# A fused attention and gated-MLP decode step: output rows spread over 128 partitions, value tiles loaded one place later, one store per queue, fifteen tiny loads

## The chip, the cores and the metric

The kernel runs on one core of a Trainium2 chip. The metric is the time of one execution on the device in microseconds (us). Three runs of the kernel before took 204.35, 204.86 and 204.87 us, median 204.86. The profile is of one execution whose span is 204.9 us. All times in this document count from the start of that span unless something else is said.

## What is computed

Eight tokens (B = 8) go through a layer norm. From the result `xn` two branches are made and multiplied, and the input is added:

```python
def A(x, k_cache, v_cache, wq, wo):     # attention, window W = 2048 of Sk = 8192
    q = (x @ wq)                        # 32 heads of 128
    k, v = the last W rows of the caches, 8 heads, each shared by 4 query heads
    p = softmax(q k^T * 128 ** -0.5)
    return (p v) @ wo
def B(x, w_gate, w_up, w_down):
    return (sigmoid(x @ w_gate) * (x @ w_up)) @ w_down
xn = layernorm(x)
out = x + A(xn) * silu(B(xn))           # [8, 1, 512], bf16
```

The bytes decide the size of the job. The windows of the two caches are 2 x 8 tokens x 8 heads x 2048 rows x 256 B = 67 MB, the weights another 14 MB. The profile counts 81.01 MB read from HBM.

## The kernel before

**Loads.** Nearly all loads are issued from SP's queue (`q0`), in one fixed order. A list `todo` holds them, and `pump` issues the head of the list while its pool has a free buffer: `kpool` with 5 buffers (tag "k") and `vpool` with 4 (tag "v"). `free(tag)` gives a buffer back after the last instruction that reads it, and pumps. The order is: `w_gate`, `w_up`, `w_down` (in the v pool, 1792 KB each), two halves of `wq` (in the k pool, 2 MB each), and then the cache tiles. A cache tile is 2 MB: one token, four heads, 128 partitions of 16 KB. There are 16 key tiles and 16 value tiles (two for each token); here they are called k0 to k15 and v0 to v15. The constant `AHEAD` (L165) places value tile n behind key tile n + AHEAD. With AHEAD = 3 the order is k0 k1 k2 k3 v0 k4 v1 ... k15 v12 v13 v14 v15. Last comes `wo`, 4 MB, 32 rows of 1 KB for each partition, in five loads: rows 0 to 4 by `load_side` (L110), and rows 5-14, 15-22, 23-28 and 29-31 by `load_rows` (L97). `load_side` views its 128 rows as 8 x 16, with the 8 outermost, so partition p holds another block of `wo` than in the other four loads. The work after it makes up for that, see below.

The framework gives DMAs from SP and ACT eight completion semaphores in turn. A DMA that takes a semaphore again first waits, on its issuing queue, until the DMA eight places before it has landed completely.

**Compute.** For each token, 16 steps (`k_transposes`, L392) turn the key tiles by TensorE (L401) and copy them out of PSUM by VectorE (L406). `scores` (L413) multiplies them with the query. `row_max`, `stat_rows`, `spread_max` and `p_transposes` make the softmax one token later, `values` (L514) multiplies with the value tiles two tokens later, and `combine`, `normalise` (L541) and `turn` (L571) bring each token's attention output into the layout that the last product needs, three tokens later. The order on TensorE is written by hand in `tasks` (L586 to L608): with 16 half steps for each token, the values of tile 0 of token b - 2 stand in half steps 1 to 8 of token b, those of tile 1 in half steps 7 to 14. So v(2b - 4) is multiplied while k(2b) is turned. After the loop stands a tail for the last tokens (L610 to L637), and then `fin` (L641): 128 matmuls of 128x128 with the rows of `wo` in order, into four blocks of 32 PSUM partitions. Two VectorE operations (L656, L658) multiply with the gate and add x, and four stores (L660) write the result.

**Layouts that the change touches.** `Z` = 32 is the block of partitions for each quarter j of the 512 output columns. In the kernel before, token b's output row is partition 32 j + b: the 8 tokens are the first 8 of 32. `hT_sb`, `oP_sb` and the identity `ident[:B, :Z]` carry this layout. In `normalise` two VectorE operations write the same product in two orders, `oB` for rows 5 to 31 and `oA` for rows 0 to 4 (the `load_side` rows), and `turn` has one matmul for each.

Of the kernel before, what the change touches and what calls it, by code (L numbers as in the profile page):

```python
# [10 lines left out]
def kernel(  # L11
# [13 lines left out]
    nc = tc.nc  # L25
    P = 128
    B, _, D = A_x.shape
    _, Hkv, Sk, Dh = A_k_cache.shape
    Hq = A_wq.shape[1] // Dh
# [19 lines left out]
    bf16 = mybir.dt.bfloat16  # L49
    f32 = mybir.dt.float32  # L50
    AF = mybir.ActivationFunctionType
    ALU = mybir.AluOpType
# [5 lines left out]
    kpool = ctx.enter_context(tc.tile_pool(name="kpool", bufs=5))  # L58
# [3 lines left out]
    consts = ctx.enter_context(tc.tile_pool(name="consts", bufs=1))  # L62
    work = ctx.enter_context(tc.tile_pool(name="work", bufs=1))
    small = ctx.enter_context(tc.tile_pool(name="small", bufs=2))
# [16 lines left out]
    q0, q1 = nc.sync, nc.scalar  # L81
    k_tiles = {}
    v_tiles = {}
    room = {"k": 5, "v": 4}
# [12 lines left out]
    def load_rows(w, tag, per, r0, r1, name):  # L97
        t = pools[tag].tile([P, r1 - r0, w.shape[1]], bf16, name=name, tag=tag)
        q0.dma_start(  # L99
            out=t[:], in_=w.rearrange("(p r) n -> p r n", r=per)[:, r0:r1, :]  # L100
        )
        return t
# [1 line left out]

    A = 8
    SD = 5

    def load_side(w, per):  # L110
        t = kpool.tile([P, SD, w.shape[1]], bf16, name="wo_sb", tag="k")
        q0.dma_start(
            out=t[:].rearrange("p r n -> p (r n)"),
            in_=w.rearrange("(e a r) n -> a e (r n)", a=A, r=per)[
                :, :, : SD * w.shape[1]
            ],
        )
        return t

    weights = {}  # L120
    todo = []

    def later(tag, f):
        todo.append((tag, f))
# [11 lines left out]
    def want_rows(name, w, tag, per, r0, r1):  # L136
        def f():
            t = load_rows(w, tag, per, r0, r1, name)
            for r in range(r0, r1):
                weights[(name, r)] = t[:, r - r0, :]  # L140

        later(tag, f)
# [4 lines left out]

        later(tag, f)

    def want_side():  # L150
        def f():
            t = load_side(A_wo, RT)
            for r in range(SD):
                weights[("wo_sb", r)] = t[:, r, :]

        later("k", f)

    RT = 32
    want_rows("wg_sb", B_w_gate, "v", KT, 0, KT)
    want_rows("wu_sb", B_w_up, "v", KT, 0, KT)  # L160
    want_rows("wd_sb", B_w_down, "v", FT, 0, FT)
    for i in range(2):
        want_rows("wq_sb", A_wq, "k", KT, 2 * i, 2 * i + 2)
    order = [(b, i) for b in range(B) for i in range(NQ)]
    AHEAD = 3  # L165
    for n in range(len(order) + AHEAD):
        if n < len(order):
            want_cache(k_tiles, A_k_cache, "k", *order[n])
        if n >= AHEAD:
            want_cache(v_tiles, A_v_cache, "v", *order[n - AHEAD])  # L170
    want_side()
    for t0, t1 in ((SD, 15), (15, 23), (23, 29), (29, RT)):
        want_rows("wo_sb", A_wo, "k", RT, t0, t1)

    x_bf = work.tile([B, D], bf16, name="x_bf")
# [3 lines left out]
    ident = consts.tile([P, P], bf16, name="ident")  # L179
# [8 lines left out]
        out=perm[:].rearrange("k (l p) -> k l p", l=G),  # L188
        in_=ident[:].rearrange("k (p l) -> k l p", l=G),
# [13 lines left out]
        out=rstd[:], in_=mv[:, 1:2], func=AF.Sqrt, bias=eps_t[:], scale=1.0  # L203
# [4 lines left out]
        out=xn_bf[:],  # L208
        in0=x_f[:],
# [7 lines left out]
    for kt in range(KT):  # L217
        nc.tensor.transpose(
            out=xnT_ps[:, kt, :],
            in_=xn_bf[:].rearrange("b (p kt) -> b kt p", kt=KT)[:, kt, :],  # L220
# [4 lines left out]

    Z = 32
    NB = D // P


    M0 = Z - rep  # L230
# [5 lines left out]
    hT_sb = work.tile([P, FT, Z], bf16, name="hT_sb")  # L236
    nc.vector.memzero(hT_sb[:])
    oP_sb = work.tile([P, RT, Z], bf16, name="oP_sb")
    nc.vector.memzero(oP_sb[:])

    NDQ = Dh // RT
    band = consts.tile([P, NDQ], bf16, name="band")
    pick = consts.tile([P, RT], bf16, name="pick")
    with nc.allow_low_precision(reason="zeros and a one"):
        nc.vector.reduce_sum(
            out=band[:], in_=ident[:].rearrange("k (q t) -> k q t", t=RT), axis=AX.X
        )
        nc.vector.reduce_sum(
            out=pick[:], in_=ident[:].rearrange("k (q t) -> k t q", t=RT), axis=AX.X
# [5 lines left out]
    for k in range(F // FC):  # L255
        g_ps = ps_t.tile([B, FC], f32, name="g_ps", tag="t")
        for kt in range(KT):
            nc.tensor.matmul(  # L258
                g_ps[:],
                lhsT=xnT_sb[:, kt, :],  # L260
                rhs=weights[("wg_sb", kt)][:, k * FC : (k + 1) * FC],
                start=(kt == 0),
                stop=(kt == KT - 1),
# [7 lines left out]
    for k in range(F // FC):  # L271
        u_ps = ps_t.tile([B, FC], f32, name="u_ps", tag="t")
        for kt in range(KT):
            nc.tensor.matmul(
                u_ps[:],
                lhsT=xnT_sb[:, kt, :],
                rhs=weights[("wu_sb", kt)][:, k * FC : (k + 1) * FC],
                start=(kt == 0),
                stop=(kt == KT - 1),
            )  # L280
        nc.vector.tensor_tensor(
            out=h_bf[:B, k * FC : (k + 1) * FC],
            in0=sigs[k],
            in1=u_ps[:],
            op=ALU.mult,
        )
    free("v")
    hT_ps = ps_m.tile([P, FT, B], bf16, name="hT_ps", tag="m")
    for t in range(FT):
        nc.tensor.transpose(  # L290
            out=hT_ps[:, t, :],
            in_=h_bf[:B, :F].rearrange("b (p t) -> b t p", t=FT)[:, t, :],
            identity=ident[:B, :B],
        )
    nc.vector.tensor_copy(out=hT_sb[:, :, :B], in_=hT_ps[:])

    b_ps = ps_s.tile([P, P], f32, name="b_ps", tag="s")
    for t in range(FT):
        for j in range(NB):
            nc.tensor.matmul(  # L300
                b_ps[Z * j : Z * (j + 1), :],
                lhsT=hT_sb[:, t, :],
                rhs=weights[("wd_sb", t)][:, j * P : (j + 1) * P],
                start=(t == 0),
                stop=(t == FT - 1),
# [9 lines left out]
    x4_ps = ps_m.tile([P, P], f32, name="x4_ps", tag="m")  # L315
    for j in range(NB):
        nc.tensor.matmul(
            x4_ps[Z * j : Z * (j + 1), :],
            lhsT=ident[:B, :Z],
            rhs=x_bf[:, j * P : (j + 1) * P],  # L320
            start=True,
            stop=True,
            tile_position=(0, Z * j),
            skip_group_check=True,
        )
# [5 lines left out]
    for h in range(Hq):  # L331
        for kt in range(KT):
            nc.tensor.matmul(  # L333
                qT_ps[:, h * B : (h + 1) * B],
                lhsT=weights[("wq_sb", kt)][:, h * Dh : (h + 1) * Dh],
                rhs=xnT_sb[:, kt, :],
                start=(kt == 0),
                stop=(kt == KT - 1),
            )
    for g in range(Hkv):  # L340
        nc.vector.tensor_copy(  # L341
            out=qm_sb[:, :, g, M0 : M0 + rep],
            in_=qT_ps[:, rep * g * B : rep * (g + 1) * B].rearrange(
                "p (hh b) -> p b hh", hh=rep
            ),
# [11 lines left out]
    for i in range(NQ):  # L357
        nc.vector.tensor_copy(
            out=turn_rows[:].rearrange("k (i j l r) -> k i j l r", i=NQ, j=NJ, l=G)[
                :, i  # L360
            ],
            in_=ident[:].rearrange("k (l j i r) -> k i j l r", i=NQ, j=NJ, l=G)[:, i],
        )
        nc.vector.reduce_sum(
            out=sel_den[:, i * Hh : (i + 1) * Hh].rearrange("k (l r) -> k l r", l=G),
            in_=ident_f[:].rearrange("k (l j i r) -> k i l r j", l=G, j=NJ, i=NQ)[:, i],
            axis=AX.X,
        )
    for e in range(2):
        nc.vector.reduce_sum(  # L370
            out=sel_out[:, e, :].rearrange("k (i h) -> k i h", i=NQ),
            in_=ident_f[:].rearrange(
                "k (i m e h) -> k e i h m", i=NQ, m=NJ // 2, e=2
            )[:, e],
# [9 lines left out]
    oT_ps = [m_ps[:, x, 168 : 168 + Hq] for x in range(2)]  # L384
    oP_ps = [m_ps[:, x, 200 : 200 + RT] for x in range(2)]
# [5 lines left out]
    row = {}  # L391
    inv = {}  # L392
# [148 lines left out]
    def normalise(b):  # L541
        o = row.pop(b)
        for e in range(2):
            nc.tensor.matmul(  # L544
                oT_ps[b % 2],
                lhsT=o[:, e, :],
                rhs=sel_out[:, e, :],
                start=(e == 0),
                stop=(e == 1),
            )  # L550

        HA = A // NDQ
        oB = small.tile([P, Hq * NDQ], bf16, name="oB")
        oA = small.tile([P, Hq * NDQ], bf16, name="oA")
        f = inv.pop(b)
        for to in (
            oB[:].rearrange("p (e s q) -> p e s q", s=HA, q=NDQ),
            oA[:].rearrange("p (s q e) -> p e s q", s=HA, q=NDQ),
        ):
            nc.vector.tensor_tensor(  # L560
                out=to,
                in0=oT_ps[b % 2]
                .rearrange("p (e s) -> p e s", s=HA)
                .unsqueeze(3)
                .to_broadcast([P, Hq // HA, HA, NDQ]),
                in1=f[:].rearrange("p (e s) q -> p e s q", s=HA),
                op=ALU.mult,
            )
        row[b] = oB, oA

    def turn(b):  # L571
        oB, oA = row.pop(b)
        for t, t0, t1 in ((oB, SD, RT), (oA, 0, SD)):
            nc.tensor.matmul(  # L574
                oP_ps[b % 2][:, t0:t1],
                lhsT=t[:],
                rhs=pick[:, t0:t1],
                start=True,
                stop=True,
            )  # L580
        nc.scalar.copy(out=oP_sb[:, :, b], in_=oP_ps[b % 2])  # L581

    for b in range(B):
        pb = b - 1 if b >= 1 else None
# [56 lines left out]
    def fin(t0, t1):  # L641
        for t in range(t0, t1):
            for j in range(NB):
                nc.tensor.matmul(  # L644
# [11 lines left out]
    nc.vector.tensor_tensor(out=prod[:], in0=gg_sb[:], in1=fin_ps[:], op=ALU.mult)  # L656
    y_bf = work.tile([P, P], bf16, name="y_bf")
    nc.vector.tensor_tensor(out=y_bf[:], in0=prod[:], in1=x4_f[:], op=ALU.add)  # L658
    for j in range(NB):
        (q0, q1)[j % 2].dma_start(  # L660
            out=out.flatten_outer_dims()[:, j * P : (j + 1) * P],
            in_=y_bf[Z * j : Z * j + B, :],
        )


# [28 lines left out]
```

## Time and profile before

| what | value |
|---|---|
| median of 3 runs | 204.86 us (204.35 to 204.87) |
| the profiled execution | span 204.9 us, from the first to the last instruction |
| HBM read | 81.01 MB, 395 GB/s over the span |
| DMA queue of SP | 6072 packets, 81.01 MB, 95.2% of 16 DMA engines' span |
| TensorE matmul busy | 164.6 us (80%) |
| VectorE busy | 128.1 us (63%) |
| ScalarE busy | 37.9 us (18%) |
| last `fin` matmul ends, issue of the last store ends | 201.5 us, 202.9 us |

How to read it: the share of a DMA queue is the time its packets took, over 16 engines times the span. Every load of 128 partitions is cut into 16 equal parts, one for each DMA engine, and each engine reports its own landing. So the trace has, beside the instructions, 16 landing times for one load; where this document says "the first engine" and "the last engine" of a load, it means the earliest and the latest of these.

### The profile page before, as it was taken

The numbers are of one execution on the slowest core, as the hardware profiler recorded it, in microseconds if no ns is written. First come the engines' busy times: TensorE is split into PE (matmuls) and PEld (weight loads), VectorE is DVE, ScalarE is ACT, GpSimd is POOL, SyncE is SP. The second block draws the span as 40 slices with busy tenths as digits, with TensorE's granted clock in tenths as the row PEclk, the third lists the DMA queues.
The fourth block names the chain that finished last, engine by engine and source line by source line (L and its number), as shares of the span: only waits on it lengthen the run. The fifth ranks groups of instructions, "written<-read, shape, count | busy, mean of one in ns | idle before, by whom it ended". The sixth has DMA issues, their size and how long they took to land.

```text
span 204.9 us, 5273 instructions
## 1 busy us (share of the span) xinstructions
PE 164.6 (80%) x2374; PEld 112.4 (55%) x2374; DVE 128.1 (63%) x246; ACT 37.9 (18%) x97; POOL 1.3 (1%) x9
## 2 busy tenths in 40 slices
PE   0496067999789989998969898999698998778542
PEld 0144066777656656566646665666466665457431
DVE  4824007899788678677947795778277967704201
ACT  5130000002501500510060006001500060070100
POOL 2000000000000000000000000000000000000000
PEclk9999555999999999999999999999799999999855
DMA  6999999999999999999999999999999999999940
GB/s 225 423 442 427 432 419 438 425 427 432 429 435 413 441 422 432 429 429 438 419 432 432 419 440 414 441 419 429 438 419 438 425 435 419 390 345 239 352 170 5
DMA packets 6141, 81.34 MB, mean 397 GB/s; under 512 B 736, under 2 KB 744, under 8 KB 1128
## 3 DMA queue, kind: packets, MB, share of 16 engines
q1 hardware_dynamic: 6072, 81.01, 95.2%
q8 instruction: 18, 0.29, 0.5%
q14 instruction: 3, 0.02, 0.0%
q10 hardware_dynamic: 48, 0.01, 0.0%
HBM read 81.01 MB, written 0.01 MB: 395 GB/s over the span
## 4 chain that ended last, share of the span: by engine, by line
DMA 54%; PE 36%; DVE 4%; ACT 2%; SPq 1%; issue 1%
DMA k_sb<-in_A_k_cache_dram 43%; PE kT_ps L401 20%; DMA wo_sb<-in_A_wo_dram 11%; PE o_ps L520 6%; PE s_ps L420 5%; PE pT_ps L483 3%; DVE kT_sb L406 3%; ACT p_buf L469 2%; SPq L99 1%; PE m_ps L500 1%; ACT L469 1%; PE m_ps L544 0%; PE m_ps L455 0%; DVE own L493 0%; DVE st L435 0%
## 5 line engine op out<-in xcount | busy, mean ns | idle before, releaser
L406 DVE COPY kT_sb<-kT_ps 128x1024 bf16<-128x1024 bf16 x128 | 87.5, 696 | 27.0 <-PE kT_ps L401 25.3
L401 PE MATMUL kT_ps<-perm,k_sb 128*128 128x128 bf16 x1024 | 79.4, 225 | 6.0 <-DMA k_sb<-in_A_k_cache_dram 6.0
L401 PEld LDWEIGHTS <-k_sb 128*128 128x128 bf16 x1024 | 60.6, 101 | 27.7 <-issue 20.5
L520 PE MATMUL o_ps<-v_sb,pT_sb 128*32 128x256 bf16 x512 | 41.1, 278 | 0.3 <-DVE pT_sb L488 0.3
L420 PE MATMUL s_ps<-kT_sb,qm_sb 128*32 128x512 bf16 x256 | 26.0, 397 | 0.5 <-DVE kT_sb L406 0.5
L520 PEld LDWEIGHTS <-pT_sb 128*32 128x32 bf16 x512 | 18.0, 96 | 9.2 <-issue 1.5
L469 ACT ACTIVATE p_buf<-s_ps,nb 32x512 bf16<-32x512 f32 x32 | 21.7, 678 | 0.5
L488 DVE COPY pT_sb<-pT_ps 128x1024 bf16<-128x1024 bf16 x16 | 10.9, 686 | 8.5 <-PE pT_ps L483 8.5
L483 PE MATMUL pT_ps<-turn_rows,p_buf 128*128 128x128 bf16 x128 | 10.9, 230 | 2.7 <-ACT p_buf L469 2.7
L463 ACT COPY nb<-m_ps 128x1 f32<-128x1 f32 x8 | 1.3, 160 | 60.6 <-PE m_ps L455 60.6
L536 ACT COPY o_sb<-o_ps 128x256 f32<-128x256 f32 x8 | 3.0, 372 | 51.0 <-PE o_ps L520 51.0
L483 PEld LDWEIGHTS <-p_buf 128*128 128x128 bf16 x128 | 9.2, 150 | 4.6 <-ACT p_buf L469 3.2
L420 PEld LDWEIGHTS <-qm_sb 128*32 128x32 bf16 x256 | 6.6, 93 | 7.5 <-issue 0.9
L333 PE MATMUL qT_ps<-xnT_sb,wq_sb 128*128 128x8 bf16 x128 | 3.7, 168 | 7.1 <-DMA wq_sb<-in_A_wq_dram 7.1
L258 PE MATMUL g_ps<-wg_sb,xnT_sb 128*8 128x448 bf16 x16 | 5.4, 526 | 3.1 <-DMA wg_sb<-in_B_w_gate_dram 3.1
L581 ACT CAST oP_sb<-m_ps 128x32 bf16<-128x32 f32 x8 | 2.4, 301 | 29.0 <-PE m_ps L574 25.2
L333 PEld LDWEIGHTS <-wq_sb 128*128 128x128 bf16 x128 | 3.6, 104 | 7.3 <-DMA wq_sb<-in_A_wq_dram 7.3
L644 PE MATMUL fin_ps<-wo_sb,oP_sb 128*32 128x128 bf16 x128 | 4.4, 309 | 3.8 <-DMA wo_sb<-in_A_wo_dram 3.3
L341 DVE CAST qm_sb<-qT_ps 128x32 bf16<-128x32 f32 x8 | 0.9, 183 | 10.2 <-PE qT_ps L333 10.2
L500 PE MATMUL m_ps<-own,ones_sq 128*128 128x32 f32 x16 | 3.3, 287 | 4.7 <-DVE own L493 4.6
L500 PEld LDWEIGHTS m_ps<-own,ones_sq 128*128 128x128 f32 x16 | 2.4, 188 | 7.1 <-DVE own L493 7.1
L644 PEld LDWEIGHTS <-oP_sb 128*32 128x32 bf16 x128 | 3.3, 138 | 4.7 <-issue 4.2
(68 smaller groups left out, 83.3 us busy)
## 6 DMA issues: line engine op xcount, KB each, us to landing
k_sb<-in_A_k_cache_dram SPq DMA_DIRECT2D x16, 2048.0 KB, 29.7
v_sb<-in_A_v_cache_dram SPq DMA_DIRECT2D x16, 2048.0 KB, 22.7
wq_sb<-in_A_wq_dram SPq DMA_DIRECT2D x2, 2048.0 KB
wg_sb<-in_B_w_gate_dram SPq DMA_DIRECT2D x1, 1792.0 KB, 7.3
wu_sb<-in_B_w_up_dram SPq DMA_DIRECT2D x1, 1792.0 KB, 11.1
wd_sb<-in_B_w_down_dram SPq DMA_DIRECT2D x1, 1792.0 KB
wo_sb<-in_A_wo_dram SPq DMA_DIRECT2D x1, 1280.0 KB, 19.3
wo_sb<-in_A_wo_dram SPq DMA_DIRECT2D x1, 1024.0 KB
```

The lines of the kernel that those rows point to most:

```text
L258: nc.tensor.matmul(g_ps[:], lhsT=xnT_sb[:, kt, :], rhs=weights[("wg_sb", kt)][:, k * FC : (k + 1) * FC], start=(kt == 0), stop=(kt == KT - 1),
L333: nc.tensor.matmul(qT_ps[:, h * B : (h + 1) * B], lhsT=weights[("wq_sb", kt)][:, h * Dh : (h + 1) * Dh], rhs=xnT_sb[:, kt, :], start=(kt = ...
L401: nc.tensor.transpose(out=kT_ps[:, c, :], in_=k_sb[:, j * CU + h * CH + c, :], identity=perm[:],)
L406: nc.vector.tensor_copy(out=kT[(b, u)][:, h * CH : (h + 1) * CH, :], in_=kT_ps[:])
L420: nc.tensor.matmul(s_ps[b][NR * l : NR * (l + 1), :], lhsT=qm_sb[:, b, i * G + l, o : o + Z], rhs=t[:, :, PG * l : PG * (l + 1)], start=(u ...
L469: nc.scalar.activation(out=p_buf[b % 2][rows, :, l, :], in_=s[rows, :].rearrange("k (c p) -> k p c", p=PG), func=AF.Exp, bias=nb[rows, :], ...
L483: nc.tensor.transpose(out=pT_ps[:, c, :], in_=p_buf[b % 2][:, :, :, h * CH + c].rearrange("k p l -> k (p l)"), identity=turn_rows[:],)
L488: nc.vector.tensor_copy(out=pT[b][:, h * CH : (h + 1) * CH, :], in_=pT_ps[:])
L500: nc.tensor.matmul(den_ps[b % 2], lhsT=ones_sq[:], rhs=own[:], start=True, stop=True)
L520: nc.tensor.matmul(o_ps[rows, b % 2, :].rearrange("k (e d) -> k e d", e=2), lhsT=pT[b][:, c, rows], rhs=v[:, m, c], start=(c == 0), stop=( ...
L536: nc.scalar.copy(out=o[:], in_=o_ps[:, b % 2, :].rearrange("k (e d) -> k e d", e=2))
L644: nc.tensor.matmul(fin_ps[Z * j : Z * (j + 1), :], lhsT=oP_sb[:, t, :], rhs=weights[("wo_sb", t)][:, j * P : (j + 1) * P], start=(t == 0), ...
```

## The change

Five edits:

- `load_side` is gone. `wo` comes in four loads of 12, 9, 7 and 4 rows, all by `load_rows`. `normalise` writes one order (`oB`), with one VectorE operation where there were two, and `turn` has one matmul where there were two.
- The tokens' output rows are spread: token b of quarter j stands on partition 32 j + 4 b, where it was 32 j + b (`SB` = 4). A small constant `spread` takes the place of `ident[:B, :Z]`.
- With that, quarters j and j + 1 are one pattern of 16 partitions with step 4, and each of the two queues (SP and ACT) issues one store of 2 x 8 x 128 where it issued two of 8 x 128.
- AHEAD is 4: the order of the tiles is k0 k1 k2 k3 k4 v0 k5 v1 ... k15 v11 v12 v13 v14 v15.
- Fifteen new loads, called probes here, stand in SP's order between the second half of `wq` and k0. Probe n reads n rows of 16 n elements (32 B for n = 1, 15 rows of 480 B for n = 15) into a tile that nothing reads.

```diff
-    A = 8
-    SD = 5
-    def load_side(w, per):
...
+    probe = [work.tile([n, 16 * n], bf16, name=f"probe{n}") for n in range(1, 16)]
+    def load_probes():
+        for n, t in enumerate(probe, 1):
+            q0.dma_start(out=t[:], in_=A_wq[:n, : 16 * n])
+    room["p"] = 1
+    later("p", load_probes)
     order = [(b, i) for b in range(B) for i in range(NQ)]
-    AHEAD = 3
+    AHEAD = 4
...
-    want_side()
-    for t0, t1 in ((SD, 15), (15, 23), (23, 29), (29, RT)):
+    for t0, t1 in ((0, 12), (12, 21), (21, 28), (28, RT)):
         want_rows("wo_sb", A_wo, "k", RT, t0, t1)
...
+    SB = Z // B
+    spread = consts.tile([B, B, SB], bf16, name="spread")
+    nc.vector.memzero(spread[:])
+    nc.vector.tensor_copy(out=spread[:, :, 0], in_=ident[:B, :B])
...
-    nc.vector.tensor_copy(out=hT_sb[:, :, :B], in_=hT_ps[:])
+    nc.vector.tensor_copy(out=hT_sb[:, :, ::SB], in_=hT_ps[:])
...
-            lhsT=ident[:B, :Z],
+            lhsT=spread[:].rearrange("k b s -> k (b s)"),
...
+        oB = small.tile([P, Hq, NDQ], bf16, name="oB")
+        nc.vector.tensor_tensor(
+            out=oB[:],
+            in0=oT_ps[b % 2].unsqueeze(2).to_broadcast([P, Hq, NDQ]),
+            in1=inv.pop(b)[:],
+            op=ALU.mult,
+        )
+        row[b] = oB
...
+        nc.tensor.matmul(
+            oP_ps[b % 2],
+            lhsT=row.pop(b)[:].rearrange("p s q -> p (s q)"),
+            rhs=pick[:],
...
-        nc.scalar.copy(out=oP_sb[:, :, b], in_=oP_ps[b % 2])
+        nc.scalar.copy(out=oP_sb[:, :, SB * b], in_=oP_ps[b % 2])
...
-    for j in range(NB):
-        (q0, q1)[j % 2].dma_start(
-            out=out.flatten_outer_dims()[:, j * P : (j + 1) * P],
-            in_=y_bf[Z * j : Z * j + B, :],
+    for j, q in ((0, q0), (2, q1)):
+        q.dma_start(
+            out=out.flatten_outer_dims().rearrange("b (j n) -> j b n", j=NB)[j : j + 2],
+            in_=y_bf[Z * j : Z * (j + 2) : SB, :],
```

More of the change, by code (lines that the diff above doesn't have):

```diff
@@ L102, in load_rows @@
         return t
-    A = 8
-    SD = 5
-    def load_side(w, per):
[L111 to L118, printed above, removed]
     weights = {}
@@ L148, in want_cache @@
         later(tag, f)
[L150 to L156, printed above, removed]
     RT = 32
@@ L550, in normalise @@
             )
[L552 to L569, printed above, removed]
-    def turn(b):
[L572 to L580, printed above, removed]
-        nc.scalar.copy(out=oP_sb[:, :, b], in_=oP_ps[b % 2])
+        oB = small.tile([P, Hq, NDQ], bf16, name="oB")
[6 more added lines that the diff above has]
+        row[b] = oB
+    def turn(b):
+        nc.tensor.matmul(
+            oP_ps[b % 2],
+            lhsT=row.pop(b)[:].rearrange("p s q -> p (s q)"),
+            rhs=pick[:],
+            start=True,
+            stop=True,
+        )
+        nc.scalar.copy(out=oP_sb[:, :, SB * b], in_=oP_ps[b % 2])
     for b in range(B):
```

## The prediction

> **What bounds the kernel now.** I read the page's slices first, then the busy time by stretches, then SP's own waits, then the chain and the timeline of the end.
>
> ```profile
> DMA  6999999999999999999999999999999999999940
> GB/s 225 423 442 427 432 419 438 425 427 432 429 435 413 441 422 432 429 429 438 419 432 432 419 440 414 441 419 429 438 419 438 425 435 419 390 345 239 352 170 5
> ```
>
> The DMA engines are busy from the first slice to the last but one. So until about 175 us the stream of loads sets the time, and every microsecond in which it runs dry is a microsecond of the kernel. Only the last slices are poor. By stretches (columns: stretch, length, busy time and count of PE, PEld, DVE, ACT, POOL, granted clock, DMA share, GB/s):
>
> ```profile
> 30.00:175.00 145.00, 133.06 (x1850) 90.73 (x1847) 110.51 (x207) 27.36 (x74) 0.00 (x0) 0.97 1.01 429
> 182.50:187.00 4.50, 2.81 (x46) 2.58 (x48) 1.29 (x2) 1.71 (x5) 0.00 (x0) 1.00 1.01 226
> 187.00:190.00 3.00, 2.44 (x32) 1.75 (x30) 1.46 (x5) 0.00 (x0) 0.00 (x0) 1.00 1.01 250
> 190.00:193.00 3.00, 1.64 (x22) 1.30 (x21) 0.91 (x3) 0.67 (x2) 0.00 (x0) 1.00 0.95 341
> 198.00:201.00 3.00, 1.89 (x59) 1.49 (x59) 0.00 (x0) 0.00 (x0) 0.00 (x0) 0.50 0.06 24
> ```
>
> Two losses stand here. From 182.5 to 190 all engines are busy and move 226 to 250 GB/s where they moved 429: this is when `wo` is read, first by `load_side`. From 198 to 201 one engine of 16 works (share 0.06) and the others have finished: the last engine ends at 200.95, the first at 194.5, their mean is 197.2. The chain agrees: it ends in a load of `wo`, ten matmuls, two VectorE operations, a store.
>
> ```profile
> 177.92 23.02 DMA wo_sb<-in_A_wo_dram
> 200.95 0.04 issue
> 200.99 0.54 PE fin_ps L644 x10
> 201.53 0.02 issue
> 201.55 0.30 DVE prod L656
> 201.85 0.02 issue
> 201.87 0.29 DVE y_bf L658
> ```
>
> **The probes.** SP issues in order, and a DMA waits for the one eight places before it. That wait is seen in the trace: k3 (L89) waits for the first `wq` load.
>
> ```profile
> SPq L89 <- DMA wq_sb<-in_A_wq_dram: 16.0, 1, 16.0
> SPq L89 <- PE qT_ps L333: 9.2, 1, 9.2
> ```
>
> In the changed order, places are x, wg, wu, wd, wq0, wq1, p1 ... p15, k0. So p3 waits for x, p4 for wg, p7 for wq0, and **p8 for wq1**, the last load that is in the queue. Behind p8 stand p9 to p15 and all key tiles. So k0 can't be issued while wq1 is still landing, as it is now (at 3.50): it is issued after wq1 is complete plus eight issues. The stream runs dry once, near 27 us.
>
> Working: wq1 lands between 25.16 (first engine) and 27.05 (last). A small load's issue isn't in the trace. Nearest are the stores of 8 rows at L660, two in 0.67 us, with 0.38 from start to start:
>
> ```profile
> 202.19 0.67 SPq L660 DMA_DIRECT2D out_dram<-y_bf  x2
> ```
>
> I take 0.38 (bounds 0.30, the shortest store, and 0.65, a key tile's issue). p8 to p15 cost 8 x 0.38 = 3.0 (2.4 to 5.2), so k0 is issued at 30.1. The waits of p9 to p15 and k0 to k2 are for small loads that have landed by then (a store of 2 KB takes 1.2 from issue to landing). From an issue into an empty queue to the landing on the last engine there are two rows. wg: 7.3 us for 8 packets of 535 ns = 4.3 an engine, so 3.0 on top. v15, which also met empty engines: 7.24 on the first engine for 8 x 611 ns = 4.9, 2.35 on top. I take 3.0: k0 has landed at 30.1 + 4.9 + 3.0 = **38.0**, where it is 31.9 now. That is +6.1. The first packet comes 1.05 (wg) to 1.36 (v15) after its issue. The Trainium skill ("DMA: Bandwidth & Descriptors", Latency and other measured facts) puts the first byte of such a queue at about 0.6 us; by it the sum would be some 0.5 us less, and the measured rows decide.
>
> TensorE sits idle until 38 in place of 31.9, mostly at the granted clock of 0.50 that the rows from 20 to 30 us show; it catches up, see below.
>
> **The stream from k0 to v15.** Now, from the last landing of k0 (31.90) to that of v14 (179.87) 30 loads pass in 147.97, 4.93 each on the slowest engine. The changed order has 31 loads from k0 to v15: 152.9, so v15 has landed at **190.9**. Now it is 187.37, because v15's 4.93 have become 7.5 in the slow stretch; on that, the change gives back 2.6 of its 6.1. Buffers: AHEAD = 4 moves v(n) one place behind, so after k15 come five value tiles. v15's buffer is v11's, and now v15 is issued at 175.09 while the first engine ended v14 at 175.93, which leaves the fast engines empty for some 0.5 us. In the changed order v11 is multiplied while v12, v13 and v14 are still to be loaded (14.7 us of stream), so this gap goes; on the slowest engine it was worth nothing.
>
> AHEAD adds a wait on TensorE: k(n + 4) lands, and v(n), needed from half step 1 of that tile, lands 4.9 later. Behind the waiting `values` stand the transposes of the same tile, and behind them VectorE's copies. Busy 133.06 of 145 us, TensorE needs about 9.0 us for a tile where the stream needs 9.8 for two, so it settles 5 us later against the keys and loses no rate. After v11 (171.2) it has 7 half steps of about 1.1 us: k15 is done near 180, 9 us of softmax follow, and v15's values start near 191. If this cover is gone, every microsecond of it is one of the end.
>
> **`wo` and the end.** Without `load_side` each engine loads 256 KB at 26.5 GB/s: 9.9 us, landing at 200.8. The last engine now carries 296 KB, the 8 of `load_side` 80 KB more than the other 8 (8 landings stand in the trace). On top comes what the slow stretch keeps. Bounds: nothing, as in `wq` (the same 32 KB between partitions, 16 KB packets at 611 ns, full rate), or all of it: 10 KB packets took 655 ns at the median where 385 is their best, and v15 lost 2.6. The new first load has 12 KB packets, a third of the way from 10 to 16 KB. I take two thirds of the ratio, 1.47 x 460 ns, for half the packets, since the slowest engine comes 3 to 4 us behind: 4 x 0.22 = 0.8. And 0.4 for half a 16 KB instruction fetch (18 on the page), each of which sets an engine back by 0.8: the last engine had three from k0 to v14, another may have one more. Last landing: 200.8 + 0.8 + 0.4 = **202.0**.
>
> Behind it: 204.9 - 200.95 = 3.95 now. The last load carries 16 matmuls in place of 12, 4 x 0.054 = +0.2. One store each queue in place of two: the second is issued 0.38 later and lands 0.4 later, -0.4; its rows cost +0.1 if they go on few engines (8 packets of 15 ns in a row). So 3.85 and **205.9**. Taken from the profiled span, 204.9, which is the median of the runs (204.86).
>
> TensorE's own floor for the end: from v15's values to `fin` 5.9 us now (187.82 to 193.72), less 0.6, since `turn` no longer waits for the second VectorE operation: 191 + 5.3 = 196.3, then 112 matmuls of 31.5 ns, 199.8. That is under 202.0, so `normalise`'s saving is covered by the loads. All else (`spread`, strided copies, seven of eight `normalise`) lies beside the stream and counts nothing; if uncovered, under 0.3 us each.
>
> **Rivals.**
>
> *The slow stretch stays.* Eight engines that enter `wo` together slow those still at v15, as now. Speaks for: at 183 us the 16 KB packets of v15, not in `wo`, also fell to 15 GB/s, so it is no matter of `load_side`'s own partitions. Against: `wq`. Price: 2.6 on v15 and 8 x 0.32 = 2.6 on the 12 KB packets, in place of my 0.8: 208 (half) to 210.3. Say 209.
>
> *Faster: the stall puts all engines back in step.* Now the last engine starts k0 1.9 late and has that at the end. After the stall all start together. If the engines that fetches hit aren't those that start late, k0's 3.0 on top becomes 2.35 or less, no fetch is extra, and `wo` runs at full rate: 204.0, and 203.0 with a whole microsecond less lag. It decides from a last landing below 200.4. The floor above, 199.8 + 0.9 + 3.3, forbids much under 203.
>
> *The probes cost nothing* (the change stalls nothing). Then k0 flows as now: 202.0 - 6.1 = 195.9, and TensorE's floor near 196: 199.5. Against: the order of SP's queue and its wait. The Trainium skill ("DMA: Bandwidth & Descriptors", Issuing engines are not separate DMA queues) calls the time to initiate a DMA usually small against the DMA itself; by that rule this rival holds. It would need eight loads in the queue behind the probes, and there are none.
>
> **How the numbers follow.** Forecast 205.9 (204.5 to 207.2) 0.46; slow stretch stays 0.28; engines in step 0.21; probes free 0.05. The range, 203.0 to 209.3, leaves out the last and the outer part of the second. A measurement can tell about 0.3% here, 204.25 to 205.47. Faster: all of the free probes and most of the third case, 0.24. Same: the lower part of the forecast and the rest of the third, 0.20. Slower: 0.56.
>
> **What would show it.** SP waits for `wq` near 27 and issues k0 near 30; the slices hold a gap of some 5 us there; k0's first transposes stand near 38. v15 lands near 191 with no gap before it; `wo` at over 400 GB/s to its end; the engines' last landings within 4 us. Wrong if the gap is under 3 us, if `wo` is read at 250 GB/s again, or if TensorE is still at work on k15 after 182.

## The result and the profile after

The changed kernel takes 208.34 us (median of 4 runs, 207.95 to 208.57), the kernel before 204.87 us (median of 4, 204.35 to 204.92). The ratio is 1.0177, with a 95% interval of 1.0158 to 1.0195: 3.5 us slower, where the prediction said 205.9, 1.0 us slower. The time lies inside the range on record and the direction is the forecast's, but the size of the change is not. The profiled execution has a span of 206.7 us and a time of 208.45 us. Keep that pair in mind; it is where most of the missing 2.4 us comes from.

The slices of the page of the changed kernel (each digit or number is one fortieth of the span):

```profile
PEclk9999555579999999999999999879999999999695
DMA  6999808999999999999999999999999999999950
GB/s 212 436 442 417 372 13 349 441 422 438 420 428 431 428 431 425 434 425 434 425 431 428 428 431 423 433 425 434 425 434 419 441 419 441 412 415 421 417 245 5
```

There is a hole in the sixth slice, 13 GB/s, that the kernel before does not have. At the far end the 390, 345, 239 and 352 GB/s of the kernel before have become 412 to 421. So one loss was added and one removed. By stretches (length, busy time and count of PE, PEld, DVE, ACT, POOL, granted clock, DMA share, GB/s):

```profile
25.00:27.00 2.00, 0.00 (x0) 0.00 (x0) 0.00 (x0) 0.00 (x0) 0.00 (x0) 0.50 0.09 35
27.00:32.00 5.00, 3.52 (x126) 3.44 (x126) 1.36 (x13) 0.00 (x0) 0.00 (x0) 0.50 0.22 60
182.50:187.00 4.50, 4.01 (x61) 2.90 (x61) 1.45 (x5) 1.07 (x4) 0.00 (x0) 1.00 1.00 404
187.00:190.00 3.00, 1.48 (x27) 1.15 (x22) 0.00 (x0) 2.84 (x9) 0.00 (x0) 1.00 0.99 418
190.00:193.00 3.00, 2.72 (x33) 2.01 (x33) 1.29 (x2) 0.00 (x0) 0.00 (x0) 0.68 1.01 425
193.00:195.00 2.00, 2.00 (x20) 1.30 (x16) 0.00 (x0) 0.00 (x0) 0.00 (x0) 0.63 0.97 411
```

The hole is SP's doing. Its timeline, its waits (total, times, longest) and two pieces of the chain say so:

```profile
3.29 26.73 SPq L147 DMA_DIRECT2D probe<-in_A_wq_dram  x15
30.07 4.18 SPq L89 DMA_DIRECT2D k_sb<-in_A_k_cache_dram  x5
```
```profile
SPq L147 <- DMA wq_sb<-in_A_wq_dram: 9.7, 2, 5.1
SPq L147 <- DMA wg_sb<-in_B_w_gate_dram: 4.1, 1, 4.1
```
```profile
29.64 0.38 SPq L147
30.07 8.29 DMA k_sb<-in_A_k_cache_dram
```

Fifteen loads that move 40 KB together hold SP for 26.73 us. The last wait is for the second half of `wq`, which lands at 27.03; the eight remaining probe issues follow and take 2.98 us together; k0 is issued at 30.07, its first packet moves at 31.6 and its last engine lands at 38.36. The end of the chain, in order of time:

```profile
190.31 0.70 DVE pT_sb L478
191.06 3.57 PE o_ps L510 x16
...
199.88 0.31 ACT oP_sb L559
200.22 2.70 PE fin_ps L622 x128
202.95 0.30 DVE prod L634
203.28 0.29 DVE y_bf L636
```

There is no `wo` in it. All 128 last matmuls run in one piece: the last of `wo` had landed at 200.97, before the matmuls that need it. In this execution TensorE, not the loads, ends last. The chain shows too where TensorE met the stream for the last time: it waited for v11.

```profile
143.94 27.69 DMA v_sb<-in_A_v_cache_dram
171.67 0.41 PE o_ps L510 x8
...
182.62 0.40 PE s_ps L410 x4
```

The last of these lines is the last scores of k15.

### The profile page after: what moved, and what is told of

It reads as the page before. It is cut to its first block, busy times and chain, and to the rows that moved or that the text cites. A ratio compares the mean times of both kernels' runs of the same rounds, so it can differ in the third digit from the quotient of the medians.

```text
span 206.7 us, 5264 instructions
## 1 busy us (share of the span) xinstructions
PE 165.6 (80%) x2366; PEld 112.2 (54%) x2366; DVE 124.8 (60%) x240; ACT 37.9 (18%) x97; POOL 1.3 (1%) x9
## 4 chain that ended last, share of the span: by engine, by line
DMA 61%; PE 29%; DVE 3%; SPq 2%; ACT 2%; issue 1%; DVEq 0%
DMA v_sb<-in_A_v_cache_dram 45%; PE kT_ps L391 13%; DMA wq_sb<-in_A_wq_dram 12%; PE o_ps L510 7%; DMA k_sb<-in_A_k_cache_dram 4%; PE s_ps L410 3%; PE pT_ps L473 2%; DVE kT_sb L396 2%; ACT p_buf L459 1%; PE fin_ps L622 1%; SPq L147 1%; SPq L99 1%; PE m_ps L534 1%; PE m_ps L490 1%; DVE pT_sb L478 0%
## 5 line engine op out<-in xcount | busy, mean ns | idle before, releaser
L510 PE MATMUL o_ps<-v_sb,pT_sb 128*32 128x256 bf16 x512 | 42.8, 288 | 3.8 <-DMA v_sb<-in_A_v_cache_dram 3.5
L510 PEld LDWEIGHTS <-pT_sb 128*32 128x32 bf16 x512 | 18.6, 99 | 15.5 <-issue 7.5
L478 DVE COPY pT_sb<-pT_ps 128x1024 bf16<-128x1024 bf16 x16 | 10.9, 686 | 8.5 <-PE pT_ps L473 8.5
L473 PE MATMUL pT_ps<-turn_rows,p_buf 128*128 128x128 bf16 x128 | 10.9, 229 | 2.7 <-ACT p_buf L459 2.7
L459 ACT ACTIVATION_READ_ACCUMULATOR p_buf<-s_ps,nb 32x1 f32 x32 | 5.9, 184 | 0.0
L425 DVE TENSOR_REDUCE st<-s_ps 128x1 f32<-128x512 f32 x8 | 5.5, 682 | 0.5 <-PE s_ps L410 0.5
```

The source lines that it names most:

```text
L425: nc.vector.reduce_max(out=st[b][:], in_=s_ps[b][:], axis=AX.X)
L459: nc.scalar.activation(out=p_buf[b % 2][rows, :, l, :], in_=s[rows, :].rearrange("k (c p) -> k p c", p=PG), func=AF.Exp, bias=nb[rows, :], ...
L473: nc.tensor.transpose(out=pT_ps[:, c, :], in_=p_buf[b % 2][:, :, :, h * CH + c].rearrange("k p l -> k (p l)"), identity=turn_rows[:],)
L478: nc.vector.tensor_copy(out=pT[b][:, h * CH : (h + 1) * CH, :], in_=pT_ps[:])
L510: nc.tensor.matmul(o_ps[rows, b % 2, :].rearrange("k (e d) -> k e d", e=2), lhsT=pT[b][:, c, rows], rhs=v[:, m, c], start=(c == 0), stop=( ...
```

## The experiments

Each kernel was compared with the kernel before on the same chip. Times are medians; ratios are to the kernel before, with their 95% interval. My theory was the prediction's: the stall on SP's queue costs about 6, the form of the side load had cost most of that before, the rest nothing. The rivals: the probes cost by being loads (packets and landings), not by their place in the queue; AHEAD or the store has a price of its own; the slow stretch is the price of short packets.

**One part alone: the changed kernel without the probes (`no_probes`).**

```diff
-    later("p", load_probes)
```

> The changed kernel without the fifteen probes; all else stays. Stall theory: the stream of loads no longer runs dry, k0 lands near 32 in place of 38.4, and all behind it comes 6.2 earlier: span 200.5, time some 6 us below the changed kernel, 202.2 (ratio to before 0.987). Rival, the waits on value tiles (AHEAD) make the end late: TensorE is then late by itself, and taking the probes away gives back less than 3 us: 205.5 or more. A second thing to see: the changed kernel's time stands 1.75 us above its span where that of before stands at it. If the probes make that difference, it goes with them and the time is 200.5.

Measured: 202.43 us, ratio 0.9884 (0.9842 to 0.9926). The probes cost 208.34 - 202.43 = 5.9 us, and without them the change is faster than the kernel before. (Its four runs lie in two pairs, 201.73 and 203.1, so the median is good to some 0.7 us.) k0's last landing is at 31.90, the last of `wo` at 195.22. The stretches of the stall, in this kernel:

```profile
25.00:27.00 2.00, 0.00 (x0) 0.00 (x0) 0.00 (x0) 0.00 (x0) 0.00 (x0) 0.50 1.00 426
27.00:32.00 5.00, 3.58 (x127) 3.50 (x128) 1.34 (x13) 0.00 (x0) 0.00 (x0) 0.50 0.99 423
```

**Where the wait begins: six probes, seven probes (`probes6`, `probes7`).** The eight semaphores come in turn, so with six probes k0 takes the one of wq0, with seven (`range(1, 8)`) that of wq1.

```diff
-    probe = [work.tile([n, 16 * n], bf16, name=f"probe{n}") for n in range(1, 16)]
+    probe = [work.tile([n, 16 * n], bf16, name=f"probe{n}") for n in range(1, 7)]
```

> Only probes 1 to 6 are kept. Their tiny loads still lie in the queue behind wq on 1 to 6 engines, but the last DMA that waits ahead of k0 is now p6, which waits for w_down (landed near 16.8), and k0 waits for the first half of wq (landed near 21.6), while 5 us of stream are still in the queue. Stall theory: the gap closes to under 1 us, time within 0.7 us of the kernel without probes. Rival, each tiny load costs by itself (0.4 us each on the path): 6/15 of the whole cost, some 2.4 us above the kernel without probes.

> Probes 1 to 7 are kept. k0 is now eight places behind the second half of wq and waits for its last landing (27.05), but no issue of a probe stands behind that wait. Stall theory: the gap is there but 3.0 us shorter than with fifteen: k0 issued near 27.1, landed near 35.2, time 3 us below the changed kernel and 3 us above the kernel without probes; the step from 6 to 7 probes costs some 3 us, far more than one load. Rival, each tiny load costs by itself: 7 cost 0.4 us more than 6.

Measured: 201.81 us with six, ratio 0.9853 (0.9831 to 0.9875), and 205.0 us with seven, ratio 1.002 (0.9998 to 1.0042). SP's timelines, first with six, then with seven:

```profile
21.63 10.07 SPq L89 DMA_DIRECT2D k_sb<-in_A_k_cache_dram  x5
```
```profile
27.09 4.75 SPq L89 DMA_DIRECT2D k_sb<-in_A_k_cache_dram  x5
```

With six, k0 is issued while wq1 still fills the engines, and nothing is lost. The seventh load, 7 rows of 224 B, costs 3.2 us, because k0 now waits until the second half of `wq` has landed. The eight further probes cost another 3.3 us, close to the 2.98 that their issues take. This is the sharpest test of the mechanism: the price is a step at a place, not so much for each load.

**The same loads from another queue (`probes_pool`).** The fifteen loads go from GpSimd's queue, after its constants.

```diff
-            q0.dma_start(out=t[:], in_=A_wq[:n, : 16 * n])
+            nc.gpsimd.dma_start(out=t[:], in_=A_wq[:n, : 16 * n])
...
-    room["p"] = 1
-    later("p", load_probes)
...
+    load_probes()
```

> The changed kernel with the same fifteen loads issued from GpSimd's queue, after its constants, so that SP's queue holds none of them and k0 does not stand behind them. Stall theory: the tiny loads themselves cost nothing, the time is that of the kernel without probes (202.4, within 1 us), with no gap near 27. Rival, the tiny loads upset the DMA engines wherever they come from: 204 or more.

Measured: 202.58 us, ratio 0.9889 (0.9863 to 0.9915), as without any probes. That the 5.9 us are the price of the loads themselves is out. They are not quite free from here either: from 20 to 25 us the stream moves 386 GB/s where it moves 433 without probes, and k0's last landing is at 32.93, 1.0 us later.

**The kernel before, again (`before_again`, `before_look`).** Unchanged, ten runs and later one more.

> The kernel before, unchanged, run as the others are, to have its time and its span from the same runs. If the time lies 1.7 to 2 us above the span as in the changed kernel, then the profiled execution of before (204.9) was a slow one among its own and the usual span is near 203.1; if the time equals the span, the changed kernel spends 1.75 us outside its span.

> The kernel before once more, one profile. The profiled execution on which the forecast was built ended its loads at 200.95 (span 204.9), another at 198.96 (span 202.9) with a time of 204.8. If the usual one is the second, this one ends them at 198.5 to 199.5 with a span of 202.5 to 203.5.

Measured: 204.88 us (ten runs; ratio 1.0003, 0.9986 to 1.0019) and 205.48 us (one run). The spans of the two profiled executions are 202.9 and 203.5 us. The time was 1.75 to 2.2 us above the span in every run of every kernel in this study. So the execution with a span of 204.9, on which the prediction was built, must by this have taken 206.7 or more, later than any timed run of this kernel (204.01 to 205.85). Its last `wo` landing, at 200.95, is the late part: v15 had landed at 187.37 as in the repeated kernel (187.38), the side load at 193.0 where that has 191.0. The end of the chain in the ten runs' profile:

```profile
177.58 21.38 DMA wo_sb<-in_A_wo_dram
198.96 0.04 issue
199.01 0.54 PE fin_ps L644 x12
```

In the later run the load lands at 199.59, slightly past the 199.5 expected, and these matmuls start at 199.63. So they start 1.4 to 2.0 us earlier than in the execution that was shown.

**The kernel before with the probes alone (`before_probes`).**

```diff
...
+    room["p"] = 1
+    later("p", load_probes)
```

> The kernel before with the fifteen probes alone added, between wq and k0. Stall theory: k0 lands 6.2 later and nothing gives it back, the last load lands near 205.2 where the kernel before has 199.0 in its usual executions: time 211 (ratio 1.030). Rival, the end of the kernel has slack that hides part of the stall: 208.3 or less.

Measured: 213.07 us, ratio 1.0409 (1.0385 to 1.0433), +8.4 us over the 204.62 measured beside it, and not +6.2. k0's last landing is at 37.95, as expected (+6.0). The slow stretch is there as before:

```profile
189.00:198.00 9.00, 7.34 (x110) 5.81 (x106) 2.85 (x7) 2.67 (x8) 0.00 (x0) 0.99 1.01 243
```

So the two losses add, and some 2.4 us come on top. In the profiles, against the repeated kernel before, 0.7 has come by v14's last landing (186.58, +6.8), 1.0 more by that of the side load (198.75 against 191.0, +7.8), and 0.8 in the last store. That gives places and no cause: in the kernel before alone the side load's last landing varied from 191.0 to 193.0.

**The kernel before without the side load (`before_wo4`).** `wo` in four loads of 12, 9, 7 and 4 rows; `normalise` and `turn` with one product.

```diff
-    want_side()
-    for t0, t1 in ((SD, 15), (15, 23), (23, 29), (29, RT)):
+    for t0, t1 in ((0, 12), (12, 21), (21, 28), (28, RT)):
```

> The kernel before without the side load: wo in four loads of 12, 9, 7 and 4 rows on 16 engines, one product in place of two, layout, AHEAD = 3 and four stores as before. Theory, the side load made the slow stretch: the stretch at half rate is gone, the last load lands near 195.2 in place of 199.0, TensorE's last product becomes co-critical (starts near 192.6, takes 3.6 at the lower granted clock), time 201.5 to 202.0 (ratio 0.985). Rival, the gain of the kernel without probes came from AHEAD = 4: no more than 0.5 below before.

Measured: 201.76 us, ratio 0.987 (0.9828 to 0.9911), 2.9 us under the 204.62 beside it. The slow stretch is gone, and the last of `wo` lands at 195.26, 3.7 earlier than in the repeated kernel before:

```profile
182.50:187.00 4.50, 3.12 (x49) 2.67 (x49) 1.29 (x2) 1.40 (x5) 0.00 (x0) 1.00 1.00 420
187.00:190.00 3.00, 2.55 (x35) 2.00 (x35) 1.09 (x4) 0.30 (x1) 0.00 (x0) 1.00 0.99 418
```

**Short packets or the side load's form (`before_rows5`).** The kernel before with the same five loads of 5, 10, 8, 6 and 3 rows, but the first read like the others: 128 partitions in order on 16 engines, where the side load's 8 x 16 view went to 8. `normalise` and `turn` have one product here too.

```diff
-    want_side()
-    for t0, t1 in ((SD, 15), (15, 23), (23, 29), (29, RT)):
+    for t0, t1 in ((0, 5), (5, 15), (15, 23), (23, 29), (29, RT)):
```

> The kernel before with the same five loads of wo (5, 10, 8, 6 and 3 rows), but the first one too as 128 rows in order on 16 engines, and with one product in place of two. It tells apart what in the side load makes the slow stretch. If it is its form (8 engines, blocks in another order): no slow stretch, time 201.8 as with four loads (ratio 0.986). Rival, it is the short packets of 5 and 10 KB 32 KB apart: the stretch at 226 to 250 GB/s stays, time 203.5 or more.

Measured: 201.08 us, ratio 0.981 (0.9782 to 0.9839). The packets of 5 KB are as short as before, and the rate is full, where the repeated kernel before has 229 and 261 GB/s in these stretches:

```profile
182.50:187.00 4.50, 3.78 (x56) 3.27 (x58) 1.29 (x2) 0.76 (x3) 0.00 (x0) 1.00 1.02 420
187.00:190.00 3.00, 2.40 (x35) 1.62 (x31) 1.09 (x4) 0.41 (x2) 0.00 (x0) 1.00 1.01 425
```

The packet records say the same. From 182.5 to 187 a 5 KB packet took 361 ns at the median in the repeated kernel before and 196 here, and a 16 KB packet of v15 took 1127 against 611. The second product of `normalise`, which is gone here as well, runs in the first profile for 0.7 us at 177.6 and at 188.2, while the slow packets last from 182 to 190; it does not account for them. So the form of the side load halves the rate, not the length of its packets.

**AHEAD alone, and the store alone (`ahead3`, `stores4`).** The changed kernel with AHEAD = 3, and the changed kernel with four stores of 8 spread rows.

```diff
-    AHEAD = 4
+    AHEAD = 3
```
```diff
-    for j, q in ((0, q0), (2, q1)):
-        q.dma_start(
-            out=out.flatten_outer_dims().rearrange("b (j n) -> j b n", j=NB)[j : j + 2],
-            in_=y_bf[Z * j : Z * (j + 2) : SB, :],
+    for j in range(NB):
+        (q0, q1)[j % 2].dma_start(
+            out=out.flatten_outer_dims()[:, j * P : (j + 1) * P],
+            in_=y_bf[Z * j : Z * (j + 1) : SB, :],
```

> The changed kernel with AHEAD = 3. Stall theory: the stream is the same and AHEAD shifts only when TensorE works: within 0.7 us of the changed kernel (208.3). Rival, the waits for value tiles make TensorE's end late (its last product starts at 200.2 though the last load lands at 201.0 and its first wo rows at 194.9): 206.5 or less.

> The changed kernel with four stores of 8 rows, two on each queue, from the spread rows. If the two stores of 16 rows cost more than they save (from the issue to the end of the span 3.1 in the changed kernel, 2.7 in before): 0.4 us below the changed kernel, 207.9. Rival, one store for each queue saves its issue, as forecast: 0.3 above, 208.6.

Measured: 208.15 us, ratio 1.0172 (1.0142 to 1.0203), and 208.52 us, ratio 1.0196 (1.0161 to 1.023). Neither can be told from the changed kernel's 1.0177: AHEAD has no price that these runs show, and the store's forecasts, 207.9 and 208.6, lie too close for them. The issues of the stores, in the kernel with four, in the changed kernel and in the repeated kernel before:

```profile
203.01 1.53 SPq L638 DMA_DIRECT2D out_dram<-y_bf  x2
```
```profile
203.59 0.64 SPq L638 DMA_DIRECT2D out_dram<-y_bf  x1
```
```profile
200.20 0.67 SPq L660 DMA_DIRECT2D out_dram<-y_bf  x2
```

Two stores of spread rows take 1.53 us to issue, two of neighbouring rows 0.67. Spreading the rows made the issue dearer, and one store for each queue (0.64 us) gave that back.

**No side load, and the spare buffer with the values (`wo4_k4v5`).** `before_wo4`'s kernel, with 4 key and 5 value buffers.

```diff
...
-    room = {"k": 5, "v": 4}
+    room = {"k": 4, "v": 5}
```

> The kernel before without the side load (201.8), with 5 value and 4 key buffers in place of 4 and 5, so that v15 need not wait for v11's buffer (issued near 175, while the first engine ends v14 at 176). If the gap before v15 counts: the gap goes, the last load lands 0.5 to 1.0 earlier, 201.0. Rival, TensorE's end (last product from 192.6) sets the time: no change, 201.8; or the missing key buffer starves TensorE: 203 or more.

Measured: 201.07 us, ratio 0.9813 (0.9789 to 0.9837). v15 is issued at 166.22 where it was near 175, so the fast engines no longer run empty before it. But `fin`'s end is where it was:

```profile
195.31 0.62 PE L610 MATMUL fin_ps<-wo_sb,oP_sb 128*32 128x128 bf16 x16 [0.31 <-DMA wo_sb<-in_A_wo_dram]
```

With the buffers as they were, the last 16 started at 195.30. The time is the 201.0 that was expected if the gap counts, but the last load did not land earlier (195.27 against 195.26), and the two kernels' intervals overlap: that the buffer gained anything is not shown. This kernel and the one with five loads in order are the fastest, 1.9% under the kernel before; no run tells them apart.

## Why the prediction was right and wrong

**The failed step** is the last of the sum: "Taken from the profiled span, 204.9, which is the median of the runs (204.86)." It set a span equal to a time, and the two numbers agree by chance. A span is 1.75 to 2.2 us shorter than its time. The execution shown was about 1.9 us later than a usual one, and in the stage that the change takes away, so it gave the side load's term a larger size than it has. The span that the terms add up to, 205.9, is measured as 206.2 to 206.7; read as a time it is some 1.8 us too low. In differences: the terms had the stall at +6.1, the removal of the side load at -5.1 (2.6 on v15, and 13.6 less 11.1 for `wo`), and the end at -0.1. On usual executions the removal is worth -3.7 us on the last landing, and in time -2.9 (four loads in order) or -3.8 (five).

That the sum came within 0.8 us of the span is in part luck. The last landing came 1.0 earlier than forecast, and that hid most of the 1.4 us by which TensorE ended later than the loads would have let it.

By times: the side load's removal is -2.9 (`before_wo4`); the whole change without the probes is -2.4 (202.43 against 204.86), so all the rest is +0.5, inside the intervals of both; the probes are +5.9. The sum is +3.5, and +3.5 is measured (208.34 against 204.87).

Point by point:

- **The probes' wait: right.** "p8 for wq1" and "issued at 30.1": 30.07. Eight issues at 0.38 were 2.98. k0's last landing "38.0": 38.36. The 6/7 step and the GpSimd queue show that it is the place in the queue. One reading under it was wrong: k3's 16.0 us are not this wait. Eight places before k3 stands `w_gate`, which had landed at 8.04; k3 takes the first `wq` load's buffer in the k pool and waits for that. The wait of eight places is seen in the changed kernel, where p4 waits 4.1 us for `w_gate`. The Trainium skill ("DMA: Bandwidth & Descriptors", Issuing engines are not separate DMA queues) calls the time to initiate a DMA usually small against the DMA; each issue here is 0.4 us, yet the order of the issues with their waits cost 5.9.
- **The stream to v15: right.** "190.9": 191.17, at full rate.
- **The gap before v15: wrong, and worth nothing.** "So this gap goes": without probes v15 is issued at 175.13 with AHEAD = 4, at 174.65 with AHEAD = 3 in the repeated kernel before. In the changed kernel the first landings of v14 and v15 lie 5.6 us apart, in the three profiles of the kernel before 5.7 to 6.4, and at full rate 4.9. The prediction let the earlier order free v11's buffer earlier; TensorE then followed the value tiles, later by the same place. What removed the gap is a fifth value buffer (4.9 apart), and that did not move the last landing of `wo`.
- **`wo`: the rate was right, the additions were too large.** The last landing was 200.97, where full rate alone gave 200.8. The +0.8 for a rest of the slow stretch has no cause left, since `before_rows5` shows that short packets alone do not slow the engines.
- **TensorE's floor: wrong.** "k15 is done near 180" and `fin` from 196.3: k15's last scores began at 182.62 and `fin` at 200.22 (198.30 with AHEAD = 3). That TensorE catches up with the stream was right: at 171.67 it waited for v11, and without probes all of this is 6.2 earlier, as the stream is (scores at 176.42, `fin` at 192.41). What failed is "After v11 it has 7 half steps of about 1.1 us": eight stand there, with the softmax's transposes in two of them and waits for VectorE, and from v11's landing to k15's last scores it is 11.0 us, here (171.63) and without probes (165.43). From these scores to `fin` it is 17.3 us in the repeated kernel before, 16.0 without probes and 17.6 here. The 1.6 more are the granted clock, 0.68 and 0.63 in the stretches from 190: 32 matmuls took 3.57 us where the kernel without probes needed 1.92. With AHEAD = 3 the chain ends in `wo` again, at the same time within the intervals; one profile of each does not say how often which is last.
- **The store: wrong by 0.7.** I took 0.3 off. From issue to the end of the span it is 2.7 us in the repeated kernel before and 3.1 in the changed one: the landing follows 1.7 and 2.0 after the issue on the two queues, where it was 1.2 to 1.4.

What stays open, and was not tried: whether the side load halves the rate because it goes to 8 engines, because its blocks stand in another order, or by something else of its form; and what the 2.4 us on top in `before_probes` are.

## What to carry to other kernels

Count the loads in a queue, not their bytes: a small load is dear where the wait that its turn brings falls on the last load in flight, and nothing a place earlier (six probes cost nothing, seven 3.2 us, fifteen 5.9). A profile is one execution: before building on its span, compare it with a second one, and never set a span equal to a time. For the compute floor of an end, go back to the last input that the engines wait for (v11 here), and read the length of the stage behind it from a trace: in the first profile these half steps take 10.9 us, from 165.46 to 176.39, and the prediction put 7 x 1.1.

## What the runs showed of the hardware that was not expected

- The side load, on 8 engines, slowed the whole stream, also the packets of v15 (1127 ns against 611): 223 to 261 GB/s in total, 420 with the same rows in order.
- A restarted stream takes long to flow: 1.5 us from k0's issue to its first packet, 8.3 from issue to last landing, where full rate needs 4.9.
- Stores of rows that lie 4 partitions apart, in the changed kernel and in `stores4`, took 0.64 to 0.76 us to issue and landed 1.7 to 2.1 after it; stores of neighbouring rows, in the kernel before, took 0.29 to 0.33 and landed 1.2 to 1.4 after it.
- The granted clock was 0.68 and 0.63 in the stretches from 190 in the changed kernel's profile, while TensorE was at work and on the way to finishing last; no run shows why.
